# Output rows: ScalarE or VectorE scales them and SyncE stores them, where ScalarE did both

## The chip, the cores and the metric

One NeuronCore of a Trainium2 chip runs the whole program. The metric is the device time of one execution in microseconds (us), here with 3 timed executions of the kernel before. The profiled execution is a separate record of one execution, and its own time stands beside its span below. Five engines work in parallel, each through its own list of instructions in order: TensorE (PE, matmuls), ScalarE (ACT, activations), VectorE (DVE), GpSimd (POOL) and SyncE (SP, which only issues DMAs here). ACT and POOL issue DMAs as well; PE and DVE do not.

## The reference, cut to what matters

```python
# q, k, v: (8 batches, 8 heads, 576 positions, 64), float32
scores = matmul(q, k.T) / 8;  scores = where(block(i) >= block(j), scores, -1e9)   # blocks of 64
attn = exp(scores - max);     attn = attn / (sum(attn) + 1e-9)
x = (attn @ v).transpose(0, 2, 1, 3).reshape(4608, 512)
h = x @ w_in                       # (512, 2048)
g = h * sigmoid(beta * h)          # beta: one value for each of the 2048 columns
out = g @ w_out                    # (2048, 512), float32 out: (4608, 512)
```

The kernel computes h * (1 + tanh(beta * h / 2)), which is twice g, and so scales the result of the last matmul by 0.5.

## The kernel before, in words

**Attention.** The work comes in 32 units, each two heads of one batch (four units to a batch). For a unit PE multiplies K by Q (L552) into PSUM, ACT takes the exponential into a bf16 tile `E` (L560, and L572 for the last 64 columns), DVE clears the masked corners of `E` (L566, L568), PE multiplies `E` by V with a column of ones beside it (L595), and DVE divides by the sum (L605, L613) into the tile `xq`. Q and K have to lie transposed in `QKT`. In the first two batches PE turns them. From the third batch on, SP loads Q and K of two units (five DMAs each, L512 and L515), POOL casts them to bf16 (L523), and one DMA transpose that SP issues turns both (L530). `xq` also has to be turned, into `xT`: by PE and DVE (L637, L644) for batches 0 to 4, by two DMA transposes from SP for each unit (L625) for batches 5 to 7. V is loaded by SP in six DMAs for each batch (L427, L430).

**The two matmuls behind it.** The 4608 rows of x are worked in 9 stages of 512 rows (`r`). For each of 16 slices `j` of the hidden width PE makes h (L680, four matmuls), ACT the tanh into `th` (L690), DVE the product into `gT` (L694). Then for each of 4 groups of 128 rows (`w`) PE adds up 16 matmuls (L711) in one bank of PSUM, ACT scales the bank into the tile `ost` (L722), and ACT issues the store of 128 rows of 2 KB to `out` (L728). `ost` has three buffers: an evacuation into one has to wait for the landing of the store that read it three groups earlier.

**What sets the order.** Nothing is ordered by hand. Every step is given to a planner as an operation (`P.op`), with the engines that may take it, a duration, the tiles that it holds, and a priority (smaller goes first). `Plan.schedule` (from L74) then steps through a planned time: an engine that is free takes the ready operation of the best priority whose tiles can be had. Buffers and PSUM banks are assigned as it goes. Each engine's list of instructions is what the planner gave it, in that order, and on the chip an engine stops at an instruction whose semaphores have not come, with everything that is behind it in the list.

For this change these of its rules matter:

- The engines are asked in the order PE, ACT, DVE, POOL, SP. An operation that two engines may take is left to the other one only if that one is free and has fewer ready operations:

```python
if len(o.engs) > 1:
    other = [x for x in o.engs if x != e]
    if any(eng_free[x] <= now and len([1 for q in pool if x in q.engs and q.ready <= now]) <
           len([1 for q in pool if e in q.engs and q.ready <= now]) for x in other):
        continue
```

- A load is held back in the plan while the planned transfers reach more than `BACKLOG` = 4000 ns ahead (`o.lazy`). A DMA transpose of Q and K is planned to hold SP for 1500 ns (L533), a load of Q or K for 5 * 600 ns (L519), a pair of transposes of `xq` for 1700 ns (L630).
- On SP the transposes have priority -1, and the loads of Q, K and V priorities of 0 to 31 that grow with the unit.

Of the kernel before, what the change touches and what calls it, by code (L numbers as in the profile page):

```python
# [4 lines left out]
ACT = mybir.ActivationFunctionType  # L5
# [279 lines left out]
def bass_blockwise_causal_attn__then__act_swish_beta_kernel(  # L285
# [10 lines left out]
    with es:  # L296
# [35 lines left out]
        P = Plan()  # L332
# [4 lines left out]
        def mm(n):  # L337
            return max(n / 2.4 + 3, 55.0)

        def act_t(n, ptr=0):  # L340
            return 0.833 * n + 93 + 93 * ptr

        def dve_t(n):
            return (n + 125) / 0.96

        LAG = 2
        def pr(u):
            b, c = divmod(u, NPAIR)
            return 10 * u if b < 2 else 994 + 100 * (b - LAG) + 4.9 * c

        def mk(fn):
            return lambda g, e: fn(g)
# [11 lines left out]
        for i in range(NQ):  # L364
# [3 lines left out]
            o = P.op("POOL", 200, mk(lambda g, i=i: g.memset(Vn[i][:, 4, :, 64:66], 0.0)), prio=-5)  # L368
# [6 lines left out]
        for i in range(NQ, NE):  # L375
# [4 lines left out]
                  xfer=100, dma=("d_beta", 1), prio=0.1)  # L380
# [3 lines left out]
                  deps=[bt, c2], tiles=[tb], lat=400, mode="full", prio=5)  # L384
# [22 lines left out]
        for i in range(NFILL):  # L407
# [5 lines left out]
            o = P.op("PE", 110, ff, deps=[c2, c4], tiles=[tf], lat=280, mode="full", prio=1e6)  # L413
# [5 lines left out]
        for b in range(B):  # L419
            ts, t = P.tile("Vs"), P.tile("V")  # L420
            tl[b] = t
            for h0, h1 in ([(0, 4), (4, 8)] if b == 0 else [(0, 8)]):
                vs = []
                for i in range(6):
                    def fv(g, e, ts=ts, b=b, h0=h0, h1=h1, i=i):
                        if i < 4:
# [8 lines left out]
                                   xfer=1400 * n, prio=(-50 if h0 == 0 else 3.5) if b == 0 else 4 * b + (3.5 if b < 2 else 0.5),  # L435
                                   dma=["d_V", h0, 1]))
# [3 lines left out]
                def fw(g, e, ts=ts, t=t, h0=h0, h1=h1):  # L440
                    return g.tensor_copy(Vn[t.slot][:, :, h0:h1, 0:64], Vs[ts.slot][:, :, h0:h1, :])  # L441

                o = P.op("POOL", 300 + 2140 * n, fw, deps=[*vs, *ones, *vzero], tiles=[ts, t],
                         prio=4 * b + 0.5 - 30 * (b < 1))
# [17 lines left out]
        for u in range(NU):  # L462
# [8 lines left out]
            if b < QB:  # L471

                turned = []
                for w, (nm, src) in enumerate((("Q", q), ("K", k))):
# [6 lines left out]
                    o = ld[nm, u] = P.op("SP", 420, fl, tiles=[ts], xfer=1200, prio=u, dma=["d_S", 0, 1])  # L481

                    def fn(g, e, ts=ts, tn=tn, p=p, w=w):
# [4 lines left out]
                    o = P.op("POOL" if onp else "DVE", 850 if onp else 470, fn, deps=[o], tiles=[ts, tn],  # L488
                             prio=-26 + u if onp else -1)

                    def ft(g, e, tn=tn, pt=pt, p=p, w=w):
                        for i in range(6):
# [4 lines left out]
                    o = P.op("PE", 6 * 43, ft, deps=[o, c4], tiles=[tn, pt, tt_], lat=6 * 43 + 170, mode="full",  # L497
                             prio=pr(u))
# [6 lines left out]
            elif p == 0:  # L505

                for w, (nm, src) in enumerate((("Q", q), ("K", k))):
                    ts = P.tile("ST")

                    def fl(g, e, ts=ts, src=src, b=b, c=c):  # L510
# [3 lines left out]
                             for i in range(4)]  # L514
# [4 lines left out]
                    o = ld[nm, u] = ld[nm, u + 1] = P.op("SP", 5 * 600, fl, deps=szero, tiles=[ts], xfer=3200, prio=u,  # L519
                                                         dma=["d_S5", 0, 5])  # L520
# [17 lines left out]
            for g0 in range(4):  # L538
                ps = P.tile("PP" if g0 < 3 else "P1")

                def fq(g, e, ps=ps, g0=g0, tqk=tqk, p=p):
                    blocks = {0: [(0, 0, 512, 0)], 1: [(1, 128, 576, 0), (0, 512, 576, 448)],
                              2: [(2, 256, 576, 0), (3, 384, 576, 320)], 3: [(4, 512, 576, 0)]}[g0]
                    for t, q0, q1, off in blocks:
                        m = min(128, 576 - 128 * t)
                        for h in range(2):
# [9 lines left out]
                o = P.op("PE", 220 if g0 < 3 else 60, fq, deps=cps, tiles=[ps, tqk, te],  # L556
                         lat=(220 if g0 < 3 else 60) + 200, mode="row", prio=pr(u) + .1 + .1*(g0 >= 2))
                if g0 < 3:
# [3 lines left out]
                    x = P.op("ACT", act_t(1024), fe, deps=[o], tiles=[ps, te], lat=act_t(1024) + 93, prio=0)  # L562
# [7 lines left out]
                else:  # L570
                    def fe(g, e, ps=ps, te=te):
                        return g.activation(E4[te.slot][:], PS[:, ps.slot, 0:64], ACT.Exp, scale=0.125)  # L572
                    x = P.op("ACT", act_t(64), fe, deps=[o], tiles=[ps, te], lat=act_t(64) + 93, prio=0)
# [16 lines left out]
            def fav(g, e, te=te, pa=pa, pb=pb, Tv=Tv, c=c):  # L590
                for h in range(2):
                    for i in range(5):
# [7 lines left out]
                      lat=30 * 34 + 180, mode="full", prio=pr(u)+.4)  # L600
# [16 lines left out]
            if b >= XB:  # L617
                def fy(g, e, tx=tx, c=c, b=b):
                    z = []
                    for t0, n, x0 in pieces(b):  # L620
                        if n % 128 == 0:
                            i, m = xq[tx.slot][:, t0 // 128:(t0 + n) // 128, :].rearrange("p t n -> p (t n)"), 128
                        else:
# [6 lines left out]
                               dma=[f"d_TX{n}_", 0, n]))  # L630
# [38 lines left out]
        for r in range(NRC):  # L669
            row = RC * r  # L670
            b0, b1 = row // S, (row + RC - 1) // S
            xd = [xt[4 * b + c] for b in range(b0, b1 + 1) for c in range(4)]
            tg = P.tile("gT")
            gs, hs = [], []
            for j in range(NJ):
                ph, tt = P.tile("P1"), P.tile("th")

                def fh(g, e, ph=ph, j=j, row=row):
                    for c in range(4):
                        z = g.matmul(PS[:, ph.slot, :], w_in[:, c, 128 * j:128 * j + 128], xT[:, c, row % RX:row % RX + RC],  # L680
                                     start=(c == 0), stop=(c == 3))
                    return z

                o = P.op("PE", 4 * mm(512), fh, deps=xd + [win[j // 4]], tiles=[ph, tg], lat=4 * mm(512) + 170,
                         mode="full", prio=1000 + 100 * r + j)

                hs.append(o)

                def fs(g, e, ph=ph, tt=tt, j=j):
                    return g.activation(th[tt.slot][:], PS[:, ph.slot, :], ACT.Tanh, scale=beta[:, j:j + 1])  # L690
                a = P.op("ACT", act_t(512, 1), fs, deps=[o, bC], tiles=[ph, tt], lat=act_t(512, 1) + 93, prio=0)

                def fg(g, e, ph=ph, tt=tt, tg=tg, j=j):
                    return g.scalar_tensor_tensor(out=gT[tg.slot][:, j, :], in0=th[tt.slot][:], scalar=1.0,  # L694
                                                  in1=PS[:, ph.slot, :], op0=ALU.add, op1=ALU.mult)
                gs.append(P.op("DVE", dve_t(512), fg, deps=[a], tiles=[ph, tt, tg], prio=0))

            for b in range(B):
                if any((S * b + a) // RC - RX // RC == r for a in (0, S - 1)):
                    for c in range(4):  # L700
                        xt[4 * b + c].deps += hs
            for w in range(4):
                po, to = P.tile("P1"), P.tile("ost")


                parts = [(0, NJ)] if r or w > 2 else [(4 * a, 4 * a + 4) for a in range(4)]
                o = None
                for j0, j1 in parts:
                    def fo(g, e, po=po, tg=tg, w=w, j0=j0, j1=j1):
                        for j in range(j0, j1):  # L710
                            z = g.matmul(PS[:, po.slot, :], gT[tg.slot][:, j, 128 * w:128 * w + 128], w_out[:, j, :],  # L711
                                         start=(j == 0), stop=(j == NJ - 1))
                        return z

                    n = j1 - j0
                    o = P.op("PE", n * mm(512), fo, deps=gs[j0:j1] + wout[j0 // 4:(j1 + 3) // 4] + ([o] if o else []),
                             tiles=[po, tg], lat=n * mm(512) + 170, mode="full",
                             prio=1000 + 100 * r + 16 + (w if n == NJ else 0.01 * j0 + 0.001 * w))

                def fv2(g, e, po=po, to=to):  # L720
                    if e == "ACT":
                        return g.activation(ost[to.slot][:], PS[:, po.slot, :], ACT.Copy, scale=0.5)  # L722
                    return g.tensor_scalar(out=ost[to.slot][:], in0=PS[:, po.slot, :], scalar1=0.5, scalar2=None,
                                           op0=ALU.mult)
                x = P.op("ACT", 600, fv2, deps=[o], tiles=[po, to], lat=680, prio=0)

                def fd(g, e, to=to, row=row, w=w):
                    return [g.dma_start(out[row + 128 * w:row + 128 * w + 128, :], ost[to.slot][:])]  # L728
                P.op("ACT", 500, fd, deps=[x], tiles=[to], xfer=900, dma=["d_ost", to], prio=-1)

        P.schedule()
        for o in P.ops:
# [68 lines left out]
```

The softmax here doesn't subtract the row's maximum and nothing guards it: scores larger than these inputs give would overflow.

## Time and profile before

| What | Value |
|---|---|
| Time, median of 3 | 366.62 us (366.54 to 366.9) |
| The profiled execution | 366.54 us, of which the span of the trace is 364.7 us |
| Busy: PE, ACT, DVE, POOL | 346.0, 209.2, 169.7, 74.4 us |
| Evacuation `ost` on ACT, L722 | 36 times 597 ns, the first at 68.6, the last at 361.5 us |
| Its store, issued by ACT, L728 | 36 times 0.34 us on the queue (0.338 to 0.434), landing 2.4 us after issue (2.0 to 7.0) |
| DMA transpose of Q and K by SP, L530 | 12 times 4.0 us on the queue (2.9 to 5.0), landing 6.0 us after issue (5.2 to 8.8) |
| DMA transpose of `xq` by SP, L625 | 24 times 1.26 us on the queue (1.2 to 2.1), landing 2.5 us after issue |

Busy time on an engine counts its instructions of work. Instructions that only issue a DMA are not counted as busy; they are listed with a "q" behind the engine (ACTq, SPq), and their length is the time that they held the engine's list. "Landing" runs from the start of the issue to the end of the transfer. A busy PE is not PE at its peak, as the ends of matmuls are modelled. The chain that ended last is followed back from the last instruction to what released each one.

### The profile page before, as it was taken

What the parts mean: (1) busy time and instruction counts of PE and PEld (TensorE: products, weight loads), DVE (VectorE), ACT (ScalarE), POOL (GpSimd) and SP (SyncE); (2) the same over time, 40 slices, a digit from 0 to 9 for tenths busy, and PEclk for the clock granted to TensorE, in tenths of its full rate; (3) what the DMA queues carried; (4) which work ended last, traced back from release to release, by engine and by line L of the source; (5) the groups of instructions that cost most, each with busy time, mean ns of one, the idle gap of its engine ahead of it and who ended that gap; (6) DMA issues with size and microseconds to landing.
All of it is one profiled execution on the core that took longest, in us unless ns stands there. A gap on an engine that the chain in (4) does not pass through costs nothing.

```text
span 364.7 us, 6938 instructions
## 1 busy us (share of the span) xinstructions
PE 346.0 (95%) x2797; PEld 174.3 (48%) x2797; DVE 169.7 (47%) x437; ACT 209.2 (57%) x309; POOL 74.4 (20%) x102
## 2 busy tenths in 40 slices
PE   7979999999897998999999999999999999999986
PEld 5646445544444544554545434544544444444442
DVE  2675976146404764426854066307721721730800
ACT  1563794159438787539793499249733733833711
POOL 6714523241331251440005213200000000000000
PEclk9999999999999999999999999999999999999999
DMA  8999999999799789995188998670202002002002
GB/s 189 237 210 262 183 204 207 212 243 207 185 244 227 167 185 205 248 210 72 25 177 200 213 186 173 151 151 18 47 33 86 0 31 86 0 31 86 1 31 86
DMA packets 146528, 52.05 MB, mean 143 GB/s; under 512 B 134704, under 2 KB 141888, under 8 KB 146496
## 3 DMA queue, kind: packets, MB, share of 16 engines
q1 hardware_dynamic: 134688, 37.38, 50.5%
q10 hardware_dynamic: 7584, 10.03, 8.3%
q0 software_dynamic: 4224, 4.19, 7.1%
q8 instruction: 22, 0.36, 0.5%
q14 instruction: 10, 0.08, 0.1%
HBM read 36.71 MB, written 9.44 MB: 127 GB/s over the span
## 4 chain that ended last, share of the span: by engine, by line
PE 74%; ACT 14%; DVE 3%; issue 1%
PE PS L711 34%; PE PS L680 28%; ACT E L560 8%; PE PS L595 6%; ACT th L690 5%; PE PS L552 3%; DVE gT L694 2%; PE PS L637 2%; ACT ost L722 1%; PE PS L411 1%; ACT E L572 1%; DVE xq L613 0%; DVE xT L644 0%; DVE inv L605 0%; PE PS L493 0%
## 5 line engine op out<-in xcount | busy, mean ns | idle before, releaser
L680 PE MATMUL PS<-xT,w_in 128*128 128x512 bf16 x576 | 132.4, 380 | 1.1 <-DVE xT L644 0.6
L694 DVE SCALAR_TENSOR_TENSOR gT<-th,PS 128x512 bf16<-128x512 f32 x144 | 97.4, 685 | 71.8 <-ACT th L690 71.6
L711 PE MATMUL PS<-w_out,gT 128*128 128x512 bf16 x576 | 128.0, 379 | 2.7 <-DVE gT L694 2.7
L690 ACT ACTIVATE th<-PS,beta 128x512 f32<-128x512 f32 x144 | 99.3, 710 | 32.8 <-PE PS L680 32.7
L560 ACT ACTIVATE E<-PS 128x1024 bf16<-128x1024 f32 x96 | 96.7, 1063 | 15.0 <-PE PS L552 14.8
L711 PEld LDWEIGHTS PS<-w_out,gT 128*128 128x128 bf16 x576 | 55.1, 98 | 68.5 <-DVE gT L694 3.5
L680 PEld LDWEIGHTS PS<-xT,w_in 128*128 128x128 bf16 x576 | 52.7, 98 | 65.1 <-DVE gT L694 2.1
L722 ACT ACTIVATE ost<-PS 128x512 f32<-128x512 f32 x36 | 21.5, 597 | 100.2 <-PE PS L711 100.2
L523 POOL CAST QKn<-ST 128x640 bf16<-128x640 f32 x48 | 34.6, 720 | 48.3 <-DMA ST<-in_k_dram 27.1
L552 PE MATMUL PS<-QKT 64*64 64x64 bf16 (+5 forms) x384 | 37.2, 281 | 3.8 <-ACT E L560 3.1
L441 POOL CAST Vn<-Vs 128x2560 bf16<-128x2560 f32 (+1 forms) x9 | 18.7, 2082 | 99.1 <-DMA Vs<-in_v_dram 99.1
L595 PE MATMUL PS<-Vn,E 128*128 128x65 bf16 x960 | 34.4, 193 | 2.6 <-DVE gT L694 2.0
L595 PEld LDWEIGHTS PS<-Vn,E 128*128 128x128 bf16 x960 | 31.5, 97 | 7.9 <-DVE gT L694 2.5
L613 DVE TENSOR_TENSOR xq<-PS,inv 128x320 bf16<-128x320 f32 x64 | 28.8, 484 | 0.3
L552 PEld LDWEIGHTS PS<-QKT 64*128 64x128 bf16 (+1 forms) x384 | 13.5, 95 | 29.3 <-issue 11.3
L566 DVE MEMSET E<- 64x64 uint32 x64 | 7.2, 112 | 33.3 <-ACT E L560 31.1
L644 DVE COPY xT<-PS 128x64 bf16<-128x64 bf16 (+2 forms) x44 | 10.7, 288 | 21.1 <-PE PS L637 20.8
L605 DVE RECIPROCAL inv<-PS 128x5 f32<-128x5 f32 x64 | 8.7, 174 | 23.1 <-PE PS L595 22.8
L411 PE MATMUL PS<-identF,identB 128*128 128x256 bf16 x104 | 15.5, 306 | 2.2 <-POOL identF L355 2.2
L501 DVE COPY QKT<-PS 128x576 bf16<-128x576 bf16 x16 | 11.9, 751 | 5.9 <-PE PS L493 5.7
L568 DVE MEMSET E<- 64x128 uint32 x32 | 5.3, 165 | 18.5 <-ACT E L560 17.3
L411 PEld LDWEIGHTS PS<-identF,identB 128*128 128x128 bf16 x104 | 10.7, 110 | 5.0 <-POOL identF L355 2.2
(28 smaller groups left out, 63.9 us busy)
## 6 DMA issues: line engine op xcount, KB each, us to landing
out_dram<-ost ACTq DMA_DIRECT2D x36, 256.0 KB, 2.4
Vs<-in_v_dram SPq DMA_DIRECT2D x28, 256.0 KB, 4.0
ST<-in_q_dram SPq DMA_DIRECT2D x48, 128.0 KB, 2.9
ST<-in_k_dram SPq DMA_DIRECT2D x48, 128.0 KB, 3.2
ST<-in_q_dram SPq DMA_DIRECT2D x8, 288.0 KB, 7.6
ST<-in_k_dram SPq DMA_DIRECT2D x8, 288.0 KB, 7.8
w_in<-in_moe_w_in_dram POOLq DMA_DIRECT2D x4, 512.0 KB, 12.1
w_out<-in_moe_w_out_dram POOLq DMA_DIRECT2D x4, 512.0 KB, 9.8
```

What stands on the lines that cost most here:

```text
L411: return g.matmul(PS[:, tf.slot, 0:256], identB[:], identW)
L441: return g.tensor_copy(Vn[t.slot][:, :, h0:h1, 0:64], Vs[ts.slot][:, :, h0:h1, :])
L523: return g.tensor_copy(QKn[tn.slot][:].rearrange("p a w n -> p (a w n)")[:, 640 * (2 * a + w):][:, 0:640] .rearrange("p (t h d) -> p t h d ...
L552: z = g.matmul(o, QKT[tqk.slot][r, p, 1, 128 * t:128 * t + m], QKT[tqk.slot][r, p, 0, q0:q1])
L560: return g.activation(E3[te.slot][:, g0, :, :], PS[:, ps.slot:ps.slot + 2, :], ACT.Exp, scale=0.125)
L595: z = g.matmul(o, eblk(te, t, i, h), Vn[Tv.slot][:, t, 2 * c + h, 0:65], start=(t == 0), stop=(t == i))
L613: return g.tensor_tensor(xq[tx.slot][:, :, 64 * w:64 * w + 64], a, x, ALU.mult)
L680: z = g.matmul(PS[:, ph.slot, :], w_in[:, c, 128 * j:128 * j + 128], xT[:, c, row % RX:row % RX + RC], start=(c == 0), stop=(c == 3))
L690: return g.activation(th[tt.slot][:], PS[:, ph.slot, :], ACT.Tanh, scale=beta[:, j:j + 1])
L694: return g.scalar_tensor_tensor(out=gT[tg.slot][:, j, :], in0=th[tt.slot][:], scalar=1.0, in1=PS[:, ph.slot, :], op0=ALU.add, op1=ALU.mult)
L711: z = g.matmul(PS[:, po.slot, :], gT[tg.slot][:, j, 128 * w:128 * w + 128], w_out[:, j, :], start=(j == 0), stop=(j == NJ - 1))
L722: return g.activation(ost[to.slot][:], PS[:, po.slot, :], ACT.Copy, scale=0.5)
```

## The change

Two edits to the last steps of each group of 128 rows. The evacuation with its factor of 0.5, which only ACT could take, may now be taken by ACT or DVE as the planner finds them (the function `fv2` holds both forms already: an activation with a copy on ACT, a tensor-scalar multiplication on DVE). The store is issued by SP in place of ACT; its planned duration goes from 500 to 400 ns and its priority from -1 to 0. The planner then orders the whole program anew with these values.

```diff
-                x = P.op("ACT", 600, fv2, deps=[o], tiles=[po, to], lat=680, prio=0)
+                x = P.op(("ACT", "DVE"), 600, fv2, deps=[o], tiles=[po, to], lat=680, prio=0)
 
                 def fd(g, e, to=to, row=row, w=w):
                     return [g.dma_start(out[row + 128 * w:row + 128 * w + 128, :], ost[to.slot][:])]
-                P.op("ACT", 500, fd, deps=[x], tiles=[to], xfer=900, dma=["d_ost", to], prio=-1)
+                P.op("SP", 400, fd, deps=[x], tiles=[to], xfer=900, dma=["d_ost", to], prio=0)
```

The clearing of the masked corners by DVE (L566, L568) is in the kernel before as well and stays as it is.

## The prediction

> **What bounds the kernel now.** I read the page first: the busy line and the chain that ended last.
>
> ```profile
> PE 346.0 (95%) x2797; PEld 174.3 (48%) x2797; DVE 169.7 (47%) x437; ACT 209.2 (57%) x309; POOL 74.4 (20%) x102
> PE 74%; ACT 14%; DVE 3%; issue 1%
> PE PS L711 34%; PE PS L680 28%; ACT E L560 8%; PE PS L595 6%; ACT th L690 5%; PE PS L552 3%; DVE gT L694 2%; PE PS L637 2%; ACT ost L722 1%; PE PS L411 1%; ACT E L572 1%; DVE xq L613 0%; DVE xT L644 0%; DVE inv L605 0%; PE PS L493 0%
> ```
>
> PE sets the end, helped in places by ACT. The edited step itself, ACT ost L722, is 1% of the chain. Next the chain in order of time, which says where. Columns: start, length, what.
>
> ```profile
> 206.20 0.60 ACT ost L722
> 206.79 0.38 ACT E L560
> 207.17 0.42 issue
> 207.59 1.03 ACT E L560
> ...
> 265.73 13.81 PE PS L711 x64
> 279.55 13.81 PE PS L680 x64
> ```
>
> From 265.73 us on there is only matmul, 64 at a time in 13.81 us (216 ns each), up to the last evacuation at 361.55. Nothing in that stretch waits for `ost` or its store, so the last five stages can't move. All that the change can do lies before 265 us, at the four places where the chain passes over an `ost` into exponentials (110.66, 161.14, 206.20, 242.93), and wherever a late load would stop PE.
>
> So the third view is the queue that receives the stores: the timeline of SP's DMA issues around the fourth stage. Columns: start, length on the queue, issue.
>
> ```profile
> 196.97 0.60 SPq L515 DMA_DIRECT2D ST<-in_k_dram  x1
> 197.61 2.26 SPq L512 DMA_DIRECT2D ST<-in_q_dram  x4
> 199.92 0.70 SPq L515 DMA_DIRECT2D ST<-in_q_dram  x1
> 200.66 2.56 SPq L625 DMA_TRANSPOSE xT<-xq  x2
> 203.26 2.39 SPq L512 DMA_DIRECT2D ST<-in_k_dram  x4
> 205.69 0.62 SPq L515 DMA_DIRECT2D ST<-in_k_dram  x1
> 206.36 2.72 SPq L625 DMA_TRANSPOSE xT<-xq  x2
> 209.12 3.67 SPq L530 DMA_TRANSPOSE QKT<-QKn  x1
> ```
>
> There is no free slot: each issue starts some 0.04 us after the last. The same view is full from 177.64 to 233 us. The transpose at 209.12 is for units 26 and 27; POOL had finished its operands by 201 (casts at 195.22 and 199.44, each pair 1.50 us), so it stood 8 us in SP's list for no reason but the issues ahead. It lands at the earliest after the shortest landing of its line, 5.2 us: 214.3. PE takes up unit 26 at 214.68, and the waits of the window 212 to 216 have this (us in total, times, the longest):
>
> ```profile
> PEld PS L552 <- DMA QKT<-QKn: 0.6, 1, 0.6
> ```
>
> It is the only wait of PE for a transposed Q and K in the whole trace. PE arrives there before its data: cover nil. Every us that SP loses between 177 and 209 is a us that PE loses at 214.7, unless the new order moves unit 26 back. The earlier transposes are far ahead of PE: issued at 61.55, 81.86, 87.04 and 160.88 for units that PE begins at 86.07, 106.28, 113.56 and 184.90, so 24 to 26 us less 6 of landing.
>
> **What the Trainium skill says.** "DMA: Bandwidth & Descriptors", section "Issuing engines are not separate DMA queues": DMAs from all engines run on the same 16 engines, and the choice of the issuer only saves sequencer time. So the bytes cost the same after the change and the question is whose list has time. The trace agrees on the size: 0.34 us of ACT's list for a store. The same page, "Two DMAs through the same engine are not ordered", says that within one queue of one DMA engine descriptors start in order; a store on SP's queue then stands behind loads already issued. No trace here shows that yet, the stores having a queue to themselves (landing 2.4 us, against 2.9 to 7.8 for SP's loads). "VectorE: DVE Perf Modes", section on the errata, prices an instruction from PSUM at 120 + 512 cycles of 0.96 GHz on DVE and 172 + 512 of 1.2 GHz on ACT: estimates of 658 and 570 ns. ACT's measured 597 is near.
>
> **The change part by part.**
>
> *Evacuation.* 36 of 597 ns on ACT may become up to 36 of about 0.66 us on DVE (estimate above; the nearest row, L694 with two operands of 512, is 685 ns). DVE is idle for over half the span and has 71.8 us of idle before L694 alone. In the stages after 265 us that is worth 0. Before 265 us the gain can only be at the four heads: the exponential behind `ost` starts up to 0.6 us sooner, at most 4 x 0.6 = 2.4 us. But at 206.20 PE began the matmuls for that exponential only at 206.09, and it ran at 206.69, so 0.2 us is nearer: 4 x 0.2 = 0.8 us. And the rule on shared work asks ACT first and gives way only if DVE has fewer ready operations; at a head the `ost` becomes ready before the exponential does, so the tie goes to ACT and most evacuations stay there. I take 0.2 us of gain, between 0 and 2.4.
>
> *Store off ACT.* 36 x 0.34 us = 12.2 us of ACT's list. I cost this at nothing, because an exponential in flight covers it: at 206.69 and 207.59 two of them start 0.90 us apart with a store issue at 206.82 between, and without a store the chain shows pairs at 1.83 us, 0.92 each. Elsewhere the 100.2 us that ACT waits for L711 cover it. Were the cover missing it would be 4 x 0.34 = 1.4 us, inside the 2.4 above.
>
> *Store onto SP, the issue.* 20 stores (five stages) fall before 265 us. The same store took ACT 0.34; SP's shortest plain loads take 0.31, its usual ones 0.58 to 0.60. With the gap to the next, 0.4 to 0.65 us. Before 161 us they fit: SP is 14 us or more ahead. Between 177 and 209 three or four stores of the fourth stage (evacuated at 193.38, 198.39, 202.74, 206.20) go in ahead of the transpose: 3 x 0.4 = 1.2 to 4 x 0.65 = 2.6; I take 3.5 x 0.46 = 1.6 us.
>
> *Store onto SP, the wait.* In the kernel before, nothing on SP depended on the second matmul; now each store holds the list until `ost` is written. Behind it stand loads, then POOL's casts, the transposes, PE's L552 and ACT's exponentials. SP ran ahead at those places, so it will be stopped there. What is late next is shown by one gap: SP stood idle from 164.86 to 177.64, waiting for `xq` of unit 20. In the trace the loads behind it had been issued by 160.1. If the last store of the third stage (`ost` written at 161.7) is put ahead of the four groups of loads that ran at 146.48 to 160.13 - the planner holds loads back, so it plausibly is - SP has after 161.7: a V load or three, 0.6 to 1.8, four groups of 2.9 = 11.6, the transpose, 4.0, together 16.2 to 17.4, which ends at 177.9 to 179.1, or later if the groups are as slow as then (13.65, ending near 181). The idle 12.8 us cover nearly all of it: lateness -0.2 to 3, I take 1.2 us.
>
> *Buffers of `ost`.* The fourth group needs the landing of the first's store. Groups come 3.45 to 5.5 us apart, so 10 us are there for a landing of 2.4 on an empty list; one transpose and two groups of loads in front would add 10. Near the limit, I take 0, up to 2.
>
> *Tail.* The last store was issued by ACT behind a semaphore from its own evacuation (361.55 + 0.60, issue at 362.18). SP waits for the same and has nothing else: 0, at most 0.2.
>
> Sum against the profiled execution (span 364.7, whole 366.54, beside a median of 366.62): -0.2 + 1.6 + 1.2 + 0 = +2.6 us, put at 0.1 more for the tail. 366.62 + 2.7 = 369.3 us. The transpose would start at about 212, land at 217 to 218, and PE would stop some 3 us at unit 26.
>
> **The rivals.**
>
> *SP becomes the bound over more than one place.* The planner charges a transpose of Q and K 1.5 us and the chip takes 4.0, so each store is reached later than planned, each load behind a store earlier than it can go. Transposes are stopped behind stores in several stages, or `ost` runs out of buffers and ACT stops with PE's bank held. Per batch SP needs some 26 us (transposes at 61.55, 87.04, 114.65, 139.58), so a stop cannot be made up fast. Two or three places of 2.5 to 3 us each: +5 to +10, about 374 us. For it: SP's full timeline. Against: 14 us of lead in the early stages.
>
> *Hidden anyway.* The new order puts the transpose ahead of the third load group or of the `xq` transposes in front of it (it is ready 8 us before its issue), or moves unit 26 back a step. Then 0 +- 0.7: 366.6 us.
>
> *Faster.* The evacuation at the heads goes to DVE and the exponentials start 0.6 us sooner at all four heads; price -2.4, with the transpose at 209 not delayed by over 0.6. 364.6 to 365.8, say 365.2 us. It decides as soon as SP's added lateness at that transpose is less than the gain at the heads. For it: ACT's 14% of the chain, and an order that is planned anew may place things better by accident. Against: the store issue is covered already and the tie rule keeps `ost` on ACT. The rewriting of the whole order is an unknown of 2 us either way in each case.
>
> **How the numbers follow.** One late place, +2.7 (own range +1 to +5): 0.42. Several places, +5 to +10: 0.25. Hidden: 0.15. Faster: 0.18. About 0.2% (0.7 us) is what a measurement of this kernel can tell from no change. Slower 0.67, within 0.15, faster 0.18. Leaving out half of the faster case and the top of the second one gives 365.0 to 376.0; the likeliest one's own range is 367.6 to 371.6.
>
> **What would show it.** Right: SP's timeline has `out` issues between 190 and 212 with hardly a gap; the transpose for units 26 and 27 issues after 211; PE's wait for QKT from DMA grows from 0.6 to 2 or more; SP's waits name an ACT or DVE `ost`; after the attention is done the 13.81 us blocks are unchanged but start later. Wrong: that wait stays under 1 us, or the time is lost in waits for a PSUM bank or `ost` buffer, or ACT's share of the chain falls with DVE carrying many evacuations.

## The result and the profile after

The changed kernel takes 368.3 us (median, 368.08 to 369.45) against 366.76 us before (366.54 to 367.03): a ratio of 1.0048, 95% interval 1.0026 to 1.0071. It is slower by about 1.5 us, inside the range forecast and with the sign forecast. The span of its profiled execution is 366.3 us.

The page of the changed kernel, its busy line and the chain that ended last:

```profile
PE 345.5 (94%) x2797; PEld 173.7 (47%) x2797; DVE 170.0 (46%) x438; ACT 208.7 (57%) x308; POOL 74.4 (20%) x102
PE 73%; ACT 12%; DVE 3%; DMA 2%; issue 1%; SPq 1%
```

The busy times have hardly moved: one instruction, a single evacuation, has gone from ACT to DVE. What is new is in the second line. DMA and SPq, SP's own list, now carry 2% and 1% of the chain; before, neither was named. The chain in order of time shows where (start, length, what):

```profile
204.81 0.60 ACT ost L722
205.41 1.83 ACT E L560 x2
207.24 0.24 ACT E L572 x2
207.48 0.29 SPq L728
207.82 0.42 SPq L512
...
210.00 0.67 DMA ST<-in_k_dram
210.68 5.71 DMA QKT<-QKn
216.44 0.75 PE PS L552 x8
...
232.39 0.56 SPq L625
232.99 2.35 DMA xT<-xq
235.39 1.08 PE PS L595 x30
```

A store on SP (L728), a group of loads (L512) and then the transpose of Q and K for units 26 and 27 set the time at which PE can go on, at 216.44. The step from ACT to SP at 207.48 is an inference of the view and not a wait that matters: the timeline below has this store already under way at 207.19. A second place follows at 235.39, where PE's multiplication by V waits until a transpose of `xq` has landed and its buffer is free. PE's waits between 205 and 245 us give the sizes (us in total, times, the longest):

```profile
PE PS L552 <- DMA QKT<-QKn: 1.8, 1, 1.8
PE PS L595 <- DMA xT<-xq: 0.9, 1, 0.9
```

In the kernel before, no matmul waited for either; only the weight load had 0.6 us. The same weight load now waits 2.3 us:

```profile
PEld PS L552 <- DMA QKT<-QKn: 2.3, 1, 2.3
```

SP's timeline ahead of the first stop:

```profile
204.59 2.56 SPq L625 DMA_TRANSPOSE xT<-xq  x2
207.19 0.58 SPq L728 DMA_DIRECT2D out_dram<-ost  x1
207.82 2.14 SPq L512 DMA_DIRECT2D ST<-in_k_dram  x4
210.00 0.63 SPq L515 DMA_DIRECT2D ST<-in_k_dram  x1
210.68 4.17 SPq L530 DMA_TRANSPOSE QKT<-QKn  x1
214.89 1.05 SPq L728 DMA_DIRECT2D out_dram<-ost  x2
```

Still no gap, and a store among the loads. It was evacuated at 197.00 and issued at 207.19, ten us later, so SP did not wait for it here. It took its slot, 0.63 us with the gap to the next issue.

To compare runs without the start of the program, which differs between executions by up to 1 us, I take from each trace the distance from the last evacuation of the second stage to the last of all. Before: 361.55 - 110.66 = 250.89 us. After: 363.16 - 110.58 = 252.58, so +1.69, close to the +1.5 of the medians. It is one execution of each kernel, but it repeats well: the five traces without a loss (the kernel before and e1, e4, e7 and e9 below) lie between 250.77 and 250.94.

### The profile page after: what moved, and what is told of

Same layout as the page of the kernel before. It is cut to its first block, busy times and chain, and to the rows that moved or that the text cites. A ratio compares the mean times of both kernels' runs of the same rounds, so it can differ in the third digit from the quotient of the medians.

```text
span 366.3 us, 6938 instructions
## 1 busy us (share of the span) xinstructions
PE 345.5 (94%) x2797; PEld 173.7 (47%) x2797; DVE 170.0 (46%) x438; ACT 208.7 (57%) x308; POOL 74.4 (20%) x102
## 4 chain that ended last, share of the span: by engine, by line
PE 73%; ACT 12%; DVE 3%; DMA 2%; issue 1%; SPq 1%
PE PS L711 33%; PE PS L680 27%; ACT E L560 8%; PE PS L595 7%; PE PS L552 3%; ACT th L690 3%; PE PS L637 2%; DVE gT L694 2%; DMA QKT<-QKn 2%; PE PS L411 1%; DMA xT<-xq 1%; DVE xq L613 1%; SPq L512 1%; ACT ost L722 0%; ACT E L572 0%
## 5 line engine op out<-in xcount | busy, mean ns | idle before, releaser
L680 PE MATMUL PS<-xT,w_in 128*128 128x512 bf16 x576 | 132.1, 380 | 1.6 <-DVE xq L613 0.6
L680 PEld LDWEIGHTS PS<-xT,w_in 128*128 128x128 bf16 x576 | 52.7, 98 | 67.0 <-DVE gT L694 3.2
L566 DVE MEMSET E<- 64x64 uint32 x64 | 7.2, 112 | 37.6 <-ACT E L560 35.9
L484 POOL CAST QKn<-ST 96x768 bf16<-96x768 f32 x12 | 10.1, 842 | 9.9 <-DMA ST<-in_q_dram 5.8
```

## The experiments

My theory: the loss comes from SP's list, in which stores stand ahead of late transposes. Its rivals: the newly planned order of the whole program is itself worse; the evacuations on DVE, or ACT's relief, count; the loss is the wait of a store and not its slot; the stores' transfers, now on SP's queue, slow the transfers there. Each ratio is against executions of the kernel before on the same chip. The edits are shown condensed. "With the lists held" means that the plan is made first, and only the named instructions then change their list or their place in it, the buffers staying as planned.

### Each edit alone

```diff
 e1: x = P.op(("ACT", "DVE"), 600, fv2, ...)     # evacuation as changed; the store stays: P.op("ACT", 500, fd, ...)
 e2: P.op("SP", 400, fd, ..., prio=0)            # store as changed; the evacuation stays: P.op("ACT", 600, fv2, ...)
```

> Only the first edit: the evacuation may go to ACT or DVE, the stores stay with ACT. The planner gives PE, POOL and SP the same lists as in the kernel before, and sends 3 of the 36 evacuations to DVE. Theory (SP's list is what costs): no store on SP, so within 0.7 us of the kernel before, 366.8, and PE's wait for the transposed Q and K stays at 0.6 us. Rival (relief of ACT matters): faster, 365 to 366. Rival (a DVE evacuation in the way costs): 367.5 or more.

> Only the second edit: stores issued by SP, every evacuation on ACT. PE's and SP's lists come out the same as in the changed kernel. Theory: the whole loss is here, 368.3 within 0.7, with PE waiting about 2 us for the transposed Q and K of units 26 and 27. Rival (the DVE evacuation costs): 366.8.

The evacuation alone: 366.54 us against 366.44 for the kernel before on that chip, ratio 1.0011 (0.9996 to 1.0026): no difference that can be told. Its trace has 250.94 us between the two evacuations, as before. The store alone: 367.93 us, ratio 1.0047 (1.0033 to 1.0060), trace 252.69: the whole loss. PE waits 1.9 us for the transpose and 0.8 us for `xq`. DVE's evacuations are out, few as they are: three in e1, all before 75 us, and one in the changed kernel. What ACT gains by losing its stores is not measured apart, since every run that takes a store from ACT gives it to SP.

### Order and queue apart

The store on SP also changes the planned order of PE (in e2 it is PE's order of the changed kernel, in e1 that of the kernel before). Two runs cross the two.

```diff
 e3 (from before) / e4 (from the changed kernel):
         P.schedule()
+        # every store: out of its list, into the list of SP (e3, at its planned start)
+        # or of ACT (e4, 70 ns after the planned end of its evacuation)
```

> The plan of the kernel before with all its lists held, except that each store is moved from ACT's list to SP's, at its planned start. PE, DVE and POOL are unchanged. Theory: the transpose for units 26 and 27 issues 2 us or more later than at 209.1, PE waits 2.5 us or more at unit 26 where it waited 0.6, and the time is 368.8 to 370.5. Rival (the new order of PE, not the queue, is the loss): 366.8 within 0.7.

> The plan of the changed kernel with all its lists held, except that each store is moved from SP's list to ACT's, behind its evacuation. PE, DVE and POOL are as in the changed kernel. Theory: the stop of PE at unit 26 shrinks by 1.5 us or more, and the time is 365.5 to 367, at or below the kernel before, since the changed order had PE 1.4 us further at 205 us. Rival (the new order is the loss): 368.3 within 0.7, like the changed kernel.

| PE's order | Stores on ACT | Stores on SP |
|---|---|---|
| as before | 250.89 us (kernel before) | 252.93 us (e3), ratio 1.0092 (1.0057 to 1.0128) |
| as after | 250.82 us (e4), ratio 1.0002 (0.9989 to 1.0015) | 252.58 us (kernel after), ratio 1.0048 (1.0026 to 1.0071) |

The times in the table are the distances in the traces, the ratios are of measured times against the kernel before. The columns differ by 2.0 and 1.8 us, the rows by 0.1 and 0.4. So it is SP's list and not the order. The old order suffers no less from stores on SP. The details of my expectation for e3 failed, though: the transpose was issued at 209.67 and not 2 us later than 209.1, and PE's wait at unit 26 is 1.4 us, less than the 2.5 I expected, with 0.6 us more at a later V multiplication. Its ratio is also higher than its trace, because three of its six executions had a low clock (last section). PE's waits for DMA in e4:

```profile
PE PS L552 <- DMA QKT<-QKn: 0.8, 1, 0.8
```

One of the two waits is about halved (by 1.0 us, where I expected 1.5 or more) and the matmuls' wait for `xq` is gone: 1.9 us in all. The fifth stage takes 37.71 us in e4 and 39.50 in the changed kernel, so the loss of 1.8 us lies there. The lead of 1.3 us that the new order has at 205 us is not a gain: e4 ends level with the kernel before. In the fifth stage the new order has 68 matmuls of L680 (counted in the trace of the changed kernel) where the old one has 60.

The transfers themselves are not slower. In e4, with the stores on ACT's queue, the last transpose of the `xq` pair that PE awaits takes 2.35 us from issue to landing, and 2.35 us in the changed kernel too (the line at 232.99 above). The transpose for units 26 and 27 takes 5.6 us in e4, 5.7 in the changed kernel and 5.0 in e2. The stores land as soon from SP's queue as from ACT's: 2.4 us at the median between 195 and 250 us, where it was 2.5 before.

### Which stores

```diff
 st = all stores in order of stages, four to a stage; lists of the changed kernel held
 e5:  st[12], st[13], st[16] on ACT, the others on SP
 e9:  the 20 of the first five stages on ACT, the 16 of the last four on SP
 e10: the 12 of the first three stages on SP, the others on ACT
 e11: the 8 of the fourth and fifth stage on SP, the others on ACT
```

> The changed kernel's plan with all its lists held, except that 3 of its 36 stores go back to ACT: the two that stand ahead of the transpose for units 26 and 27 in the fourth stage, and the first of the fifth stage, which stands ahead of four transposes of xq. Theory (the issue slots of these three are the loss): the transpose issues about 1.2 us sooner against PE, both waits shrink, and 1.0 us or more of the 1.6 is recovered: 366.3 to 367.3. Rival (the loss is lateness carried on from the stores of the earlier stages): 367.8 or more.

> The changed kernel's plan with its lists held; the 20 stores of the first five stages on ACT, the 16 of the last four on SP. Theory (only a store that stands ahead of loads and transposes costs): SP has no loads left there, so like the run with all stores on ACT, 366.2 to 366.8, and in the trace 250.8 us from the last evacuation of the second stage to the last of all. Rival (a store from SP costs at the tail or by its wait in itself): 367.5 or more.

> The same, with only the 12 stores of the first three stages on SP. They stop SP's run ahead and eat its idle time before unit 20. Theory of lateness carried on: SP is 1 us late when the fourth stage begins and the transpose for units 26 and 27 is later by that, so 0.5 to 1 us of the 1.7 is here, 366.8 to 367.5. Theory of the three slots alone: nothing is here, 366.2 to 366.7.

> The same, with only the 8 stores of the fourth and fifth stage on SP. Theory of lateness carried on: the other 0.7 to 1.2 us, 367.0 to 367.6. Theory of the slots alone: nearly all of it, 367.7 to 368.2.

| Run | Ratio to before (interval) | Trace, us |
|---|---|---|
| e9, last 16 on SP | 0.9996 (0.9987 to 1.0004) | 250.77 |
| e10, first 12 on SP | 1.0000 (0.9984 to 1.0017) | 253.86 |
| e11, middle 8 on SP | 1.0025 (1.0012 to 1.0039) | 251.95 |
| e5, all but three on SP | 1.0032 (1.0010 to 1.0055) | 251.90 |

Sixteen stores that have no load behind them cost nothing, although SP waits for nearly all of them: a wait with nothing urgent behind it is out, and so is the tail. The middle eight cost 0.25% (367.46 us), inside what lateness carried on had forecast and below what the three slots alone should give. PE's waits for DMA in e11:

```profile
PE PS L595 <- DMA xT<-xq: 1.1, 1, 1.1
PE PS L552 <- DMA QKT<-QKn: 0.9, 1, 0.9
```

SP waits for none of these eight: each is issued 2.8 us or more after its evacuation began. So this loss, 1.1 us of the 1.8 in the traces (251.95 against 250.82 of e4), comes from stores that only take their turn in the list, and it lies at `xq`. Taking three slots away recovers 252.58 - 251.90 = 0.7 us in the trace, not 1.0 or more, and the intervals of the two ratios overlap: PE's wait for the transpose falls from 1.8 to 0.6 us, but that for `xq` rises from 0.9 to 1.2. Neither of the two simple readings of e5 holds.

The early twelve are not clear. Their median of 366.11 us shows no loss, where lateness carried on had forecast 366.8 to 367.5. But four of 22 executions lie at 368.4 to 369.7 us and the others at 365.2 to 366.7, and the profiled one is among the four. In it the transposes for units 24 and 25 and for 26 and 27 are issued 1.0 and 1.9 us later against PE than in e4, so lateness is carried on there; PE then stops for 2.25 us at unit 26, and something else comes on top, the clock (last section). The four are the ones with a low clock; of 46 executions of the kernel before on that chip two were. Whether the early stores alone bring this about is left open. The parts do not add up by rule: 0 and 0.25% apart, 0.48% together.

### Where the stop goes

```diff
 e6 (stores on SP) / e7 (stores on ACT), lists of the changed kernel held:
+        # in SP's list: the transpose for units 26 and 27 ahead of the K load of units 28 and 29
+        # (and, in e6, of the store at 207.19)
```

> The changed kernel's plan with all stores left on SP; only the transpose for units 26 and 27 is moved in SP's list ahead of the one store and the K load of units 28 and 29 that stand before it. Theory: it issues 3 us sooner, PE's wait for it vanishes, and the time is 366.0 to 367.2; the wait for xq in the fifth stage stays. Rival (the stores cost through something else than this list): 368 as before the move.

> The run with the changed order and the stores on ACT, and the transpose for units 26 and 27 ahead of the K load of units 28 and 29. Theory: its PE wait of 0.8 us at unit 26 goes, 365.0 to 366.0, below the kernel before by some 0.5 us. Rival (ACT is the bound there, so an earlier transpose is worth nothing): 366.2 to 366.8.

In e6 the transpose is issued at 206.42 and PE's wait for it is gone, as expected. The time is not what I expected: 369.02 us, ratio 1.0073 (1.0047 to 1.0099), trace 252.67 against 252.58. (Three of its seven executions had a low clock; the median of the others is 368.4.) PE's waits for DMA in the same stretch of e6:

```profile
PE PS L595 <- DMA xT<-xq: 2.0, 1, 2.0
```

The wait for `xq` has doubled, from 0.9 to 2.0 us, and takes back all that was won. SP owes the same issues; the next late one stops PE in place of the first. My expectation of 366.0 to 367.2 is refuted, and with it the idea that one transpose is the loss. With the stores on ACT the same move wins nothing either: e7's trace has 250.82 us, as e4, and its time is 367.23 us, ratio 1.0027 (1.0009 to 1.0045), above both forecasts. PE's wait of 0.8 us went away and the fifth stage took 37.71 us as in e4. The rival (ACT bound there) is the likely reason: in e7 the chain runs through ACT and DVE from 204.5 to 215.7 us, where in e4 it runs through SP's list. That its median is higher than e4's comes in part from the clock, which was low in six of its 22 executions; the other 16 are still 0.7 us above the kernel before, and the one trace does not show why.

### Doubling the suspected cost, and telling the planner

```diff
 e8: -  return [g.dma_start(out[row + 128 * w:row + 128 * w + 128, :], ost[to.slot][:])]
     +  return [g.dma_start(out[... + 64 * a: ... + 64 * a + 64, :], ost[to.slot][64 * a:64 * a + 64, :]) for a in range(2)]
 e12: planned SP time: transpose of Q and K 1500 -> 4000, pair of xq transposes 1700 -> 2600, store 400 -> 620
```

> The changed kernel with each store issued as two DMAs of 64 rows, so 72 issues on SP in place of 36, the lists held otherwise. Theory: two more issues of 0.4 to 0.65 us ahead of the transpose for units 26 and 27 and some more at the xq transposes: PE's waits grow by 1 to 2.5 us, 369 to 371. Rival (issue slots on SP don't matter): 368.3 within 0.5.

> The changed kernel with the planner told what the traces show of SP's list: 4000 ns in place of 1500 for a transpose of Q and K, 2600 in place of 1700 for a pair of xq, 620 in place of 400 for a store. The whole order is planned anew. If the loss is that the planner doesn't see SP's list as full, it places PE's units after the transposes it can have, PE's waits for DMA fall below 1 us in sum, and the time is 365.5 to 367.5. If the list is full whatever the plan knows, 367.8 to 369.5.

With 72 issues in place of 36 the time is 378.07 us, ratio 1.034 (1.0295 to 1.0384), trace 261.78, +9.2 us over the changed kernel where 1 to 2.5 were expected. The bytes are the same. The direction is the theory's, the size is not: more things begin to go wrong. From the waits of the whole run, first ACT's, then PE's:

```profile
ACT ost L722 <- DMA out_dram<-ost: 6.2, 1, 6.2
PE PS L552 <- DMA QKT<-QKn: 5.2, 2, 4.0
```

An evacuation finds no free `ost` buffer, as its store of three groups earlier sits in SP's list, and ACT stops 6.2 us with the exponentials behind it; the fourth stage ends 4.5 us later than in the changed kernel (209.35 for 204.81). Then PE stops 4.0 us for a transpose and its clock falls for a while (last section); the fifth stage takes 44.13 us for 39.50. This is the rival "SP becomes the bound over more than one place", and it is as near as one more issue for each store.

Telling the planner the prices that the traces show does not help: 370.99 us, ratio 1.0123 (1.0079 to 1.0168), above both forecasts. Three of the six executions had a low clock; the other three lie at 368.7 to 369.2 us, and the trace has 253.92. PE's waits that the profile puts down to DMA fall to 0.6 and 0.4 us, as hoped. But PE has a third wait, of 1.5 us, for which the profile names no cause ("issue"):

```profile
233.44 1.06 PE L595 MATMUL PS<-Vn,E 128*128 128x65 bf16 x30 [1.54 <-issue]
```

The second pair of `xq` transposes landed at 233.35, just before it ended, so it is most likely the same wait once more, and the waits for DMA did not fall below 1 us in sum. The stretch from the last evacuation of the fourth stage to the second of the fifth takes 26.22 + 8.01 us against 23.31 + 6.06 in the changed kernel; 3.2 us of that come back by the end of the fifth stage (41.13 against 39.50 in all). No run was clearly faster than the kernel before.

## Why the prediction was right

**The end and the evacuation.** Right. From 281.16 us on the blocks are 13.81 us as before. (The stages that can't move are the last four of nine, not five.) One evacuation of 36 went to DVE, as the tie rule made likely, at 680 ns (estimate 658). The gain put at 0.2 us measures as none (e1).

**The store off ACT at nothing.** Not refuted, but tested only in part: 16 stores taken from ACT change nothing (e9), and for the 20 before 265 us, leaving ACT and entering SP's list always go together.

**SP's slots.** The price is right: each store in the full stretch takes 0.58 to 0.60 us plus 0.04, within the 0.40 to 0.65 given, though the sum used 0.46. I took 3.5 stores ahead of the transpose; two went ahead (201.10 and 207.19), two behind it at 214.89. So 2 x 0.63 = 1.3 us in place of 1.6. That these two slots make the transpose late is not shown: counted from the last evacuation of the second stage it lands at 105.81 us in the changed kernel and at 104.89 in e4, which has no store on SP, but at 104.95 in e11, which has both slots.

**SP's lateness.** Right in direction. The transpose for units 22 and 23 was issued at 175.23 and done by 179.15, inside the 177.9 to 181 worked out (from which the lateness is 0.3 to 3.4, not -0.2 to 3); SP's idle 12.8 us were used up. The first transposes came 10 to 14 us later (72.48 for 61.55, 120.57 for 107.77) and no matmul waited there, as forecast. Against e4 SP is 1.0 us late at the transpose for units 24 and 25, near the 1.2 taken. But at the next one, with two more slots in front, it is 0.8 us late and not 1.0 + 1.3: SP made up time on the way.

**The stop at unit 26.** The transpose was forecast for 212, landing at 217 to 218, with a stop of some 3 us. It was issued at 210.68, PE went on at 216.44, and the stop is 1.8 us. "Unless the new order moves unit 26 back" came about and changed nothing: PE now does 36 matmuls of L680 between the fourth stage and unit 26 where it did 28, which uses up its lead of 1.3 us, and it reaches unit 26 at 214.6 as before. From there each us of SP was a us of PE, as assumed: the transpose landed 1.8 us later against PE (105.81 for 103.97), and PE stopped 1.8 us more.

**What the sum missed.** The term that was mis-sized is SP's delay at that transpose: slots and lateness together were put at 2.8 us, and it was issued 1.6 us later than before (210.68 for 209.12, the starts differing by 0.1) and 0.8 us later than in e4. What the sum left out is a second place, `xq` in the fifth stage, 0.9 us. So the nearness of +2.7 to the measured +1.5 is in part luck: one place was priced too high and another had no price. The account that fits the runs is e4 against the changed kernel: PE's waits grow from 0.8 to 1.8 + 0.9, by 1.9 us, and the time by 1.8. How these 1.8 us divide between slots and lateness is open. e11 gives 1.1 us to the slots of the middle stores; e2 and the changed kernel have the same list on SP, and yet that transpose is issued 0.9 us apart in their traces, so single traces can't divide it finer.

**The rivals.** "Hidden anyway" named the case that the transpose goes ahead of the loads, then 0. e6 made that case and it is wrong: the loss stays. "Faster" had no part. "Several places" was right about the number of places, two and not one, and wrong about their size in this kernel, 1.8 and 0.9 us for 2.5 to 3; with twice the issues (e8) it is what happens. The terms for the buffers of `ost` and for the tail were rightly put at nothing: no evacuation of the changed kernel waits for a store, and both spans end 3.1 to 3.2 us after the last evacuation begins.

## What to carry to other kernels

A queue that is always issuing is an engine that is always busy, even if it computes nothing: look for gaps in its timeline before adding to it, and count the slots ahead of the late transfers. Where a stop is taken away by moving one item forward in such a list, ask which item is late next; here only another list with room (e4) gave all the time back. A step behind which no load stands could be put on that queue for free (e9).

## What the runs showed of the hardware

**The issue of a store.** The same store, 128 rows of 2 KB, holds SP's list for a time that depends on what stood there just before. In the trace of the changed kernel 22 of the 36 found the list idle for 0.27 us or more and took 0.33 to 0.38 us; 13 began 0.04 or 0.05 us after a load or a transpose and took 0.58 to 0.60; one right behind another store took 0.42. On ACT all 36 took 0.34 to 0.43 us.

**The clock after a stop of PE.** A stop can cost more than itself. In the profiled execution of e10 PE stopped for 2.25 us before 216.13. The views by stretch (PE's busy time first, the granted clock and the DMA share near the end) and PE's timeline around it:

```profile
210.00:215.00 5.00, 3.88 (x24) 1.52 (x20) 3.31 (x7) 5.00 (x9) 1.44 (x2) 1.00 0.88 176
215.00:220.00 5.00, 3.87 (x16) 1.29 (x16) 2.24 (x6) 3.18 (x5) 0.00 (x0) 0.71 1.14 227
...
216.13 0.76 PE L552 MATMUL PS<-QKT 64*128 64x512 bf16 x8 [2.25 <-DMA QKT<-QKn]
216.81 3.32 PE L680 MATMUL PS<-xT,w_in 128*128 128x512 bf16 x8
```

The 0.71 is a mean over 5 us: the clock granted to TensorE is 0.50 from 217.1 to 220.6 us and 1.00 around it, and eight matmuls take 3.32 us, where the kernel before has them in 1.90. In e8 the clock is 0.50 for 6.8 us from 222.4 on, while PE stands in its stop of 4.04 us (219.11 to 223.15). In both it falls 3.3 us after PE stopped. After the 1.8 us of the changed kernel it stays at 1.00, and so it did after a stop of 2.33 us in e8, so how long a stop has to be, or what else decides, is not settled.

**What this does to the medians.** The mean granted clock was recorded for every execution, not only for the profiled ones. A spell like that of e10 makes it 1 - 0.5 x 3.4 / 367 = 0.995, and within each run of the table the executions at 0.995 or less are its slowest. Of the kernel before 5 of 113 executions are among them, of the changed kernel one of four (369.45 us), of e2 and e9 none, of e8 all.

| Run | Executions at 0.995 or less | Median of the others against the kernel before's others |
|---|---|---|
| e3 | 3 of 6 | +1.7 us |
| e6 | 3 of 7 | +2.2 us |
| e7 | 6 of 22 | +0.7 us |
| e10 | 4 of 22 | -0.4 us |
| e12 | 3 of 6 | +2.4 us |

So a good part of what e3, e6, e7 and e12 lose in the median goes with the clock and not with SP's list alone. That a stop of PE brings the clock down in these executions too is likely, but only the profiled ones have a trace.
